# Attention on TensorE: all steady products in 64x32 tiles, scores and PV on opposite diagonals

## The chip, the cores and the metric

The kernel runs on one core of a Trainium2 chip. The metric is device time in microseconds (us); three runs of the kernel before gave a median of 669.69 us (669.62 to 669.82). One more execution was recorded by the hardware profiler, and all lines of a profile below come from such recorded executions. Engines are named as in the profile: PE is TensorE (PEld its weight loads), ACT is ScalarE, DVE is VectorE, POOL is GpSimd, SP is SyncE.

## The reference

```python
x  = A_x                                   # 1 x 2048 x 512, bf16
xn = layernorm(x)
q  = (xn @ wq) as 32 heads of 16;  k = xn @ wk;  v = xn @ wv     # one k and v for all heads
p  = softmax(q k^T * 16**-0.5);  s = concat_heads(p v) @ wo
g  = silu(silu(xn @ w1) @ w2)              # w1: 512 x 1792, w2: 1792 x 512
out = x + s * g
```

Each of the 32 heads has 2048 x 2048 scores. Their exponentials are the bulk of the work of the other engines, and the products around them the bulk of TensorE's.

## The kernel before, in words

**Order of work.** The kernel carries a planner (class `Planner`). A Python loop at build time holds a clock per engine, a time for each instruction and a latency for each pair of engines, and places the next instruction of the engine whose clock is earliest. `pe_step`, `act_step` and `generic_step` choose what that is. What comes out is one fixed list of instructions per engine, with semaphore waits where a buffer or an operand comes from another engine. On the chip each engine takes its list in order; the constants at the top of the file (`NPA`, `PRESS`, `A_LOW`, `SEEDS` and so on) only shape the lists.

**Scores.** The queries stand in 4 chunks of 512 and the heads in octets of 8. A q product gives `qt_sb`, 128 rows by 512 queries: 8 heads of 16 rows. A group `g` is half an octet (4 heads), 32 groups in all. `kt_sb[:, 0]` holds K with 16 live rows in each stripe of 32, `kt_sb[:, 1]` the same moved down by 16, so that a stripe's product picks one of its two heads. A score unit is one head by 128 keys by 512 queries: one matmul of 32 rows by 128 columns into a PSUM bank of its own (`s_mm`, L866). Up to four of them, in four row tiles, make a round (`do_S`). There are 2048 units. Banks 0 to 6 serve scores and other products, bank 7 (`OB`) holds the sum of PV.

**Exponentials.** A unit goes to one of two engines. ScalarE reads up to three adjoining banks in one instruction and writes exp to `pa_sb` (L1717). Or VectorE writes an integer form of the power of two to `db_sb` (L1002), from which GpSimd (L1202, four units in one instruction) or now and then VectorE (L1196) makes three shifted copies in `ds_sb`; the four copies, against four differently weighted copies of V, average out the error. So a VectorE unit costs PV four entries and a ScalarE unit one.

**PV.** An entry is 128 keys of one head: 128 rows by 32 columns (16 of V, 16 of ones for the denominator). Four heads' entries in four column tiles make a round (`do_pv`, L1282), all into bank 7. When a group's entries are done, VectorE transposes the bank (L1338), takes reciprocals and multiplies (L1341, L1342) and, after two groups, transposes back to `on_sb` (L1349).

**Products.** q, h (w1), z (w2) and w (wo) are jobs (`product`, L511): rounds of four column tiles, 128 rows by 32 columns, into one bank. A few of a job's rounds may be cut into 32x128 pieces that fill the fourth tile of a score round (L618). `gated` gives SiLU by a tanh on ScalarE (L669) and one VectorE instruction (L671). `final` and `store` end a 128-row tile of the output. The prologue transposes the normalized x (L527), makes K (`mk_K`, L553, evacuated at L565 and L567) and V (`mk_V`, L583, L592).

**Changes of form.** The planner counts `SWITCH` = 105 ns wherever TensorE passes from one tile form to another (`pe_start`). A score round ("S", 32x128) and the rounds of PV and jobs ("C", 128x32) are two forms. The last six units of the kernel are done in halves of 256 queries (`begin_halves`, L1667), so that the final normalization can begin on the first half.

```python
return pe.matmul(bank(b), lhsT=kt_sb[32 * i:32 * i + 32, g % 2, kt * P:(kt + 1) * P],      # a score unit
                 rhs=qt_sb[32 * i:32 * i + 32, (g // 2) % NQR, :],
                 start=True, stop=True, tile_position=(32 * i, 0))
...
h = pe.matmul(bank(OB)[32 * i:32 * (i + 1), cols], lhsT=lhs, rhs=rhs, start=s0, stop=s1,   # a PV entry
              tile_position=(0, 32 * i), skip_group_check=True)
```

Of the kernel before, what the change touches and what calls it, by code (L numbers as in the profile page):

```python
# [15 lines left out]
P = 128  # L16
# [5 lines left out]
SEEDS, STRETCH, SPREAD = (4812, 312, 1660, 4615, 1697, 8414, 4190, 8770, 5102, 5729), 64, 0.3  # L22
PIECE_MIN = {"z": 4, "h": 9, "q": 9, "w": 9}
# [3 lines left out]

T_P, T_SH, T_TR, T_AF = 600.0, 600.0, 630.0, 64.3
T_P64, DV_MIN, T_LIB = 1035.0, 40, 300.0
NPIECE = 1  # L30
HOLD_PO, URG_SPLIT = 300.0, 0
# [5 lines left out]


# [4 lines left out]
PH = []  # L43
# [4 lines left out]
BLG = 0  # L48
NEAR, AHEAD = 18, 0.6
SWITCH, SKEW = 105.0, 10.0  # L50
INF = float("inf")
DVE_LIMIT = 4000.0
MARGIN, MARGIN_END = 16, 20
TWO_LIMIT = 1300.0
HOLD, Q_LEAD = 1000.0, 3.3

LOW_USE, HIGH_USE, USE_WIN = 0.55, 0.8, 3000.0
S_TOL = 30.0
CLOSING, URGENT = 3, 1.5
NPA, PRESS = 26, 16  # L60
PRESS_Z, PRESS_H = 20, 16
PA_HI, DS_HI = 30, -1
NDB, NDS = 5, 8
STOL4 = 0.0
START_Z, START_H = 4, 8
EVAC = ()
LATE, QUEUE = 0.0, 10
Q3, Q4, J3, J4, N3, N4, SOLO = 10, -1, 1, 2, 1, 2, 0
END_DV = 40
RH, EVR, SC_PRIO, MT_EARLY = 6, (0, 2), 0, 1  # L70
METER, RATE, R0 = (), 1.0, 1.0
WIDE, NMIN, EARLY = 3, 3, 300.0
ONE_LIMIT = 2500.0
A_LOW, JOB_SPARE = 1000.0, 0


class Op:
    __slots__ = ("eng", "emit", "deps", "ports", "idx", "inc", "val", "t0", "end", "vis", "dma", "know", "sem", "waits", "mode", "ring")


class Task:
# [11 lines left out]
    (PE, AC): 221.0, (PE, DV): 221.0, (PE, PE): 0.0,  # L93
# [7 lines left out]
class Planner:  # L101

    def __init__(self):
        self.clk = {e: 0.0 for e in ENGINES}
        self.order = {e: [] for e in ENGINES}
        self.lastw = {}
        self.readers = {}
        self.tasks = {e: [] for e in ENGINES}
        self.mode = None
        self.dma_t = self.acc_t = 0.0  # L110
        self.last2 = {DV: None, PO: None}
# [29 lines left out]
    def place(self, eng, dur, emit, reads, writes, dma=0, t0=None, ports=1, after=None):  # L141
# [30 lines left out]
        self.order[eng].append(op)  # L172
        for k in reads:
            self.readers.setdefault(k, []).append(op)
# [5 lines left out]
    def set_mode(self, mode):  # L180
        self.mode = self.order[PE][-1].mode = mode
# [114 lines left out]
def bass_recurrent_scan__grouped_kv_mqa__dense_activation_silu__prompt_kernel(  # L296
# [20 lines left out]
    NKT = S // P  # L317
    SLOTS = 4 * NKT
# [8 lines left out]
    with ExitStack() as es:  # L327
# [12 lines left out]
        kt_sb = sb("kt_sb", [P, 2, S], BF16)  # L340
        v_sb = sb("v_sb", [P, K + 1, NKT, 48], BF16)
# [10 lines left out]
        tmp_sb = sb("tmp_sb", [P, 8, D], BF16)  # L352
# [6 lines left out]
        if EVAC:  # L359
            hs_sb = sb("hs_sb", [P, 2, NQ], BF16)  # L360
# [8 lines left out]
        zer_sb = sb("zer_sb", [P, NQ], BF16)  # L369
# [17 lines left out]
        PH.clear()  # L387
# [27 lines left out]
        pl.add(Task(DV, 550.0, lambda v: v.memset(zer_sb[:], 0.0), (), ["zer"], 0))  # L415
        pl.add(Task(DV, 435.0, lambda v: v.memset(wke_sb[:], 0.0), (), ["wke"], 0))
# [15 lines left out]
        for j in range(K + 1):  # L432
            pl.add(Task(PO, 660.0, lambda g, j=j: g.memset(v_sb[:, j, :, :], 1.0 if j == 0 else SHIFT_W[j - 1]),
                        (), [("V", j, c) for c in range(NC)], 3))
        pl.add(Task(PO, 1800.0, lambda g: g.memset(kt_sb[0:DH, 1, :], 0.0), [("xn", 3)], [("kt1", c) for c in range(NC)], 3,
                    gate=lambda: all(xn_task[t].op is not None for t in range(4))))
        pl.add(Task(AC, 1500.0, lambda a: a.activation(scr_sb[:, 0:1], scr_sb[:, 1:2], ACT.Exp), ["scr"], ["scr2"], 0))
        wke4 = wke_sb[:].rearrange("p c (i e) -> p c i e", e=32)
        pl.add(Task(AC, 300.0, lambda a: a.activation(
            wke4[:, :, :, 0:DH], wk_sb[:, :, :].unsqueeze(2).to_broadcast([P, NDC, 4, DH]), ACT.Copy),  # L440
# [59 lines left out]
        def job(kind, arg, pace, rounds, consume, preds=(), bk=None, mode="C", gate=None):  # L500
            jb = Job()
            jb.kind, jb.arg, jb.pace, jb.rounds, jb.consume = kind, arg, pace, rounds, consume
            jb.preds, jb.bank, jb.fixed, jb.mode, jb.gate = preds, bk, bk is not None, mode, gate
            jb.due, jb.pos, jb.end, jb.got, jb.left, jb.piece, jb.prev = None, 0, len(rounds), set(), len(rounds), None, None
            jb.tasks = {}
            jobs.append(jb)
            return jb
# [38 lines left out]
        def mk_K(c, ka, kb, bk=None):  # L546
# [13 lines left out]
            def consume(jb, op):  # L560
                b = jb.bank
                dst = kt_sb[:, 0, ka * P:kb * P]
                keys = [("kt0", k) for k in range(ka, kb)]
                if c == 0:
                    t = Task(AC, T_AF + 0.8333 * n, lambda a: a.activation(dst, bank(b)[:, 0:n], ACT.Copy), [("ps", b)], keys, 0)  # L565
                else:
                    t = Task(DV, T_P, lambda v: v.tensor_copy(dst, bank(b)[:, 0:n]), [("ps", b)], keys, 0)  # L567
                for k in range(ka, kb):
                    evac_kt[k] = t
                return [t]  # L570
# [5 lines left out]
        def mk_V(c):  # L576
            def rnd(k):
                def mk(b):
                    def emit(pe):
                        h = None  # L580
                        for t in (2 * k, 2 * k + 1):
                            for dc in range(NDC):
                                h = pe.matmul(bank(b)[:, t * DH:(t + 1) * DH],  # L583
                                              lhsT=xnT_sb[:, dc, (4 * c + t) * P:(4 * c + t + 1) * P],
                                              rhs=wv_sb[:, dc, :], start=(dc == 0), stop=(dc == NDC - 1))
# [4 lines left out]
            def consume(jb, op):  # L590
                b = jb.bank
                t = Task(DV, 400.0, lambda v: v.tensor_tensor(  # L592
                    v_sb[:, :, 4 * c:4 * c + 4, DH:2 * DH],
                    bank(b)[:, 0:4 * DH].rearrange("p (t e) -> p t e", e=DH).unsqueeze(1).to_broadcast([P, K + 1, 4, DH]),
                    wj_sb[:, :].unsqueeze(2).unsqueeze(3).to_broadcast([P, K + 1, 4, DH]), ALU.mult),
                    [("ps", b)] + [("wj", j) for j in range(K + 1)], [("V", j, c) for j in range(K + 1)], 0,
                    on_place=None)
# [3 lines left out]
            job("V", c, 0.0, [(rnd(k), ["wv"] + xnT_keys(c), 520.0) for k in range(2)], consume,  # L601
                bk=OB if c == 0 else None, mode="F", gate=lambda: xnT_ready(c))
# [4 lines left out]
        def product(jb, lhs, rhs, needs):  # L607
            n = len(jb.rounds)

            def rnd(k):  # L610
                def mk(b):
                    last = jb.left == 1
                    return lambda pe: col4(pe, b, lambda j: lhs(k, slice(0, P), 32 * j, 32), rhs(k, slice(0, P)), k == 0, last)
                return mk

            def piece(k, i, last):
                rows, b = slice(32 * i, 32 * i + 32), jb.bank
                return (lambda pe: pe.matmul(bank(b), lhsT=lhs(k, rows, 0, P), rhs=rhs(k, rows), start=False, stop=last,  # L618
                                             tile_position=(32 * i, 0), skip_group_check=True), needs(k))
            jb.rounds = [(rnd(k), needs(k), MM) for k in range(n)]  # L620
            jb.piece = piece

        def mk_q(oi):
            c, o = divmod(oi, NOC)

            def consume(jb, op):
# [7 lines left out]
                     gate=lambda: xnT_ready(c) and (oi < NQR or left_oct[oi - NQR] == 0))  # L634
            product(jb, lambda k, rows, a, n: wq_sb[rows, k, P * o + a:P * o + a + n],
                    lambda k, rows: xnT_sb[rows, k, c * NQ:(c + 1) * NQ], lambda k: ["wq"] + xnT_keys(c))

        def mk_q0(ta, tb, bk):
            n = (tb - ta) * P

            def rnd(t, dc):
                def mk(b):
                    def emit(pe):
                        for j in range(4):
                            h = pe.matmul(bank(b)[32 * j:32 * (j + 1), (t - ta) * P:(t - ta + 1) * P],
                                          lhsT=wq_sb[:, dc, 32 * j:32 * (j + 1)], rhs=xnT_sb[:, dc, t * P:(t + 1) * P],
# [15 lines left out]
        def gated(b, k, scale, dst, key, kind):  # L662
            src, held = bank(b), ("ps", b)
            t0 = None
            if kind in EVAC:
                src, held = hs_sb[:, k, :], ("hs", k)
                t0 = Task(DV, T_P, lambda v: v.tensor_copy(hs_sb[:, k, :], bank(b)), [("ps", b)], [held], 0,
                          [hs_last.get(k)])
            t1 = Task(AC, 490.0, lambda a: a.activation(t_sb[:, k, :], src, ACT.Tanh, scale=scale),  # L669
                      [held], [("t", k)], 0, [t0])  # L670
            t2 = Task(DV, T_P, lambda v: v.scalar_tensor_tensor(  # L671
                out=dst, in0=t_sb[:, k, :], scalar=1.0, in1=src, op0=ALU.add, op1=ALU.mult),
                [held, ("t", k)], [key], 0 if t0 is None else 1, [t1], ports=1 if t0 is None else 2)
            t2.first = [t1, t2] if t0 is None else [t0]
            if t0 is not None:
                hs_last[k] = t2
                pl.add(t1)
                pl.add(t2)
            return t2

        hs_last = {}

        def mk_h(c, ft, pace):
            def consume(jb, op):
# [3 lines left out]
                u_task[c, ft] = gated(b, k, 0.5, u_sb[:, ft, :], ("u", ft), "h")  # L688
# [6 lines left out]
        def mk_z(tt, pace):  # L695
            c, r = divmod(tt, 4)

            def consume(jb, op):
# [3 lines left out]
                tmp_task[tt] = gated(b, k, 0.25, tmp_sb[:, tt % 8, :], ("tmp", tt % 8), "z")  # L702
# [4 lines left out]
                and (tt < 8 or tt - 8 in fin_task and fin_task[tt - 8].op is not None))  # L707
# [1112 lines left out]
```

## Time and profile before

| | |
|---|---|
| median of 3 runs | 669.69 us (669.62 to 669.82) |
| span of the profiled execution | 667.9 us |
| granted TensorE clock, mean | 1.00 of full speed |
| DMA | 12.86 MB in all, mean 19 GB/s |

The span runs from the first to the last instruction. "Busy" is the time that at least one row of the engine covers; rows of one engine can overlap, since the next instruction starts before the last has left the pipeline, so a busy share says less than the distance from start to start. A group's row reads: line, engine, operation, out<-in, shape, count | busy us, mean ns of one | idle us before them, and what ended most of it. A matmul row lasts some 380 ns although the next round can start sooner.

The 40 slices show a start of some 15 us with GpSimd nearly idle, an even middle, and a short end:

```profile
DVE  8989999999899999989999899999999999998995
ACT  6999999999999999999999999999999999999997
POOL 3059889999898889998989888999899989897972
```

### The profile page before, as it was taken

How to read it: one execution, taken by the hardware profiler on the slowest of the kernel's cores; microseconds unless marked ns; L12 is line 12 of the kernel's file. 1: busy time of each engine (PE TensorE's matmuls, PEld its weight loads, DVE VectorE, ACT ScalarE, POOL GpSimd, SP SyncE). 2: the span in 40 equal slices, each digit the busy share in tenths (PEclk: the TensorE clock that was granted, in tenths of full speed). 3: DMA queues.
4: the chain of work that ended last, by engine and by line, in shares of the span. 5: the costliest groups of instructions: out<-in, count | busy, mean ns of one | idle time of the engine just before them, and what ended most of it. 6: DMA issues, size and time to landing. Idle time of an engine off the chain costs nothing.

```text
span 667.9 us, 21230 instructions
## 1 busy us (share of the span) xinstructions
PE 657.8 (98%) x8972; PEld 190.3 (28%) x8973; DVE 613.6 (92%) x1093; ACT 652.8 (98%) x767; POOL 561.9 (84%) x560
## 2 busy tenths in 40 slices
PE   8999999999999999999999999999999999999997
PEld 4322222222222222222222222222222322222222
DVE  8989999999899999989999899999999999998995
ACT  6999999999999999999999999999999999999997
POOL 3059889999898889998989888999899989897972
PEclk9999999999999999999999999999999999999999
DMA  9500000000000000000000010000000000000000
GB/s 302 164 9 2 3 1 2 2 3 2 1 2 18 19 18 18 1 2 2 2 2 2 18 32 18 2 2 2 2 2 2 2 18 18 17 18 2 2 2 33
DMA packets 11501, 12.86 MB, mean 19 GB/s; under 512 B 1808, under 2 KB 10768, under 8 KB 11408
## 3 DMA queue, kind: packets, MB, share of 16 engines
q1 hardware_dynamic: 10928, 10.78, 5.0%
q8 instruction: 72, 1.18, 0.7%
q0 software_dynamic: 192, 0.46, 0.2%
q10 hardware_dynamic: 288, 0.26, 0.1%
q14 instruction: 21, 0.17, 0.1%
HBM read 8.95 MB, written 2.10 MB: 17 GB/s over the span
## 4 chain that ended last, share of the span: by engine, by line
PE 88%; ACT 6%; DVE 4%; issue 1%; DMA 0%; ACTq 0%; DVEq 0%
PE ps L1282 38%; PE ps L866 29%; PE ps L511 20%; ACT pa_sb L1717 6%; DVE db_sb L1002 1%; DVE stats_sb L458 1%; ACT t_sb L669 1%; DMA ds_sb<-in_A_x_dram 0%; DVE fin_sb L719 0%; PE ps L527 0%; DVE xnT_sb L538 0%; DVE xn_sb L487 0%; DVE ob_sb L731 0%; DVE mv_sb L462 0%; DVE on_sb L1316 0%
## 5 line engine op out<-in xcount | busy, mean ns | idle before, releaser
L1717 ACT ACTIVATE pa_sb<-ps 128x1024 bf16<-128x1024 f32 (+2 forms) x670 | 617.0, 1027 | 4.8 <-PE ps L866 3.5
L1202 POOL INT64_ADD ds_sb<-db_sb x544 | 554.0, 1040 | 64.2 <-DVE otr_sb L1342 31.7
L1002 DVE TENSOR_SCALAR db_sb<-ps 128x512 uint16<-128x512 f32 x736 | 475.4, 683 | 40.0 <-PE ps L866 28.6
L1282 PE MATMUL ps<-ds_sb,v_sb 128*32 128x512 bf16 x2208 | 268.7, 383 | 0.0
L866 PE MATMUL ps<-qt_sb,kt_sb 32*128 32x512 bf16 x2048 | 251.2, 384 | 3.9 <-ACT pa_sb L1717 0.9
L1282 PE MATMUL ps<-pa_sb,v_sb 128*32 128x512 bf16 x1316 | 240.9, 382 | 0.0
L1282 PE MATMUL ps<-db_sb,v_sb 128*32 128x512 bf16 x736 | 169.3, 383 | 0.0
L866 PEld LDWEIGHTS ps<-qt_sb,kt_sb 32*128 32x128 bf16 x2048 | 62.8, 91 | 276.7 <-ACT pa_sb L1717 151.2
L1282 PEld LDWEIGHTS ps<-ds_sb,v_sb 128*32 128x32 bf16 x2208 | 65.6, 95 | 62.3 <-issue 44.6
L511 PE MATMUL ps<-xnT_sb,w_sb 128*32 128x512 bf16 x896 | 71.7, 383 | 0.0
L1282 PEld LDWEIGHTS ps<-pa_sb,v_sb 128*32 128x32 bf16 x1316 | 58.8, 95 | 37.9 <-issue 24.7
L511 PE MATMUL ps<-w_sb,u_sb 128*32 128x512 bf16 x820 | 64.1, 383 | 0.0
L1282 PEld LDWEIGHTS ps<-db_sb,v_sb 128*32 128x32 bf16 x736 | 42.2, 95 | 20.2 <-issue 14.7
L669 ACT ACTIVATE t_sb<-ps 128x512 bf16<-128x512 f32 x72 | 44.9, 623 | 0.0
L671 DVE SCALAR_TENSOR_TENSOR u_sb<-t_sb,ps 128x512 bf16<-128x512 bf16 x56 | 38.2, 683 | 1.0
L618 PE MATMUL ps<-w_sb,u_sb 32*128 32x512 bf16 x76 | 29.2, 384 | 0.0
L511 PEld LDWEIGHTS ps<-xnT_sb,w_sb 128*32 128x32 bf16 x896 | 17.1, 94 | 26.1 <-issue 21.1
L1359 POOL DMA_DIRECT2D kt_sb<-kt_sb x4 | 2.3, 566 | 23.9 <-DVE var_sb L481 8.1
L1338 DVE STREAM_TRANSPOSE f_sb<-ps 128x512 f32<-128x512 f32 x31 | 21.9, 706 | 0.0
L511 PEld LDWEIGHTS ps<-w_sb,u_sb 128*32 128x32 bf16 x820 | 15.2, 95 | 22.5 <-issue 19.3
L511 PE MATMUL ps<-wo_sb,on_sb 128*32 128x512 bf16 x256 | 18.9, 383 | 0.0
L511 PE MATMUL ps<-xnT_sb,wq_sb 128*32 128x512 bf16 x240 | 18.7, 384 | 0.1
(74 smaller groups left out, 180.8 us busy)
## 6 DMA issues: line engine op xcount, KB each, us to landing
w_sb<-in_B_w_dram SPq DMA_DIRECT2D x2, 1792.0 KB, 13.4
xr_sb<-in_A_x_dram SPq DMA_DIRECT2D x16, 128.0 KB, 2.6
out_dram<-ob_sb SPq DMA_DIRECT2D x16, 128.0 KB, 1.7
ds_sb<-in_A_x_dram SPq DMA_DIRECT2D x3, 512.0 KB, 6.6
wq_sb<-in_A_wq_dram SPq DMA_DIRECT2D x1, 512.0 KB, 4.9
wo_sb<-in_A_wo_dram SPq DMA_DIRECT2D x1, 512.0 KB, 16.2
kt_sb<-kt_sb POOLq DMA_DIRECT2D x4, 112.0 KB, 3.7
ds_sb<-in_A_x_dram ACTq DMA_DIRECT2D x2, 128.0 KB, 2.9
```

The lines of the kernel that those rows point to most:

```text
L458: ts_ = pl.add(Task(DV, 593.0, lambda v, t=t: v.bn_stats(stats_sb[:, t, :], x_tile(t)), [xkey(t)], [("st", t)], 1 + j, gate=(lambda j=j: S ...
L511: last = h.matmul(bank(b)[32 * j:32 * (j + 1), 0:n], lhsT=lhs(j), rhs=rhs, start=start, stop=stop, tile_position=(0, 32 * j), skip_group_c ...
L618: return (lambda pe: pe.matmul(bank(b), lhsT=lhs(k, rows, 0, P), rhs=rhs(k, rows), start=False, stop=last, tile_position=(32 * i, 0), skip ...
L669: t1 = Task(AC, 490.0, lambda a: a.activation(t_sb[:, k, :], src, ACT.Tanh, scale=scale), [held], [("t", k)], 0, [t0])
L671: t2 = Task(DV, T_P, lambda v: v.scalar_tensor_tensor(out=dst, in0=t_sb[:, k, :], scalar=1.0, in1=src, op0=ALU.add, op1=ALU.mult), [held, ...
L866: return pe.matmul(bank(b), lhsT=kt_sb[32 * i:32 * i + 32, g % 2, kt * P:(kt + 1) * P], rhs=qt_sb[32 * i:32 * i + 32, (g // 2) % NQR, :], ...
L1002: bt.P[i] = pl.add(Task(DV, T_P, lambda v: v.tensor_scalar(db_sb[:, bt.b, i * NQ:(i + 1) * NQ], bank(b), 128.0 * LOG2E, 128.0 * (SHIFT_BET ...
L1202: whole["po"].append(pl.add(Task(PO, T_P64, lambda g, cols=cols: g.int64_add(ds_sb[:, s, cols].bitcast(U64), db_sb[:, bt.b, cols].bitcast( ...
L1282: h = pe.matmul(bank(OB)[32 * i:32 * (i + 1), cols], lhsT=lhs, rhs=rhs, start=s0, stop=s1, tile_position=(0, 32 * i), skip_group_check=True)
L1338: t1 = pl.add(Task(DV, T_TR, lambda v: v.transpose(f_sb[:, k, :], bank(OB)), [("ps", OB)], [("F", k)], 1, [norm.get(("m", g - 2))]))
L1359: kt1[c] = pl.add(Task(PO, T_SWDGE, lambda e: e.dma_start(kt_sb[DH:P, 1, cols], kt_sb[0:P - DH, 0, cols]), [("kt0", k) for k in range(4 * ...
L1717: op = pl.place(AC, 0.8333 * NQ * n + T_AF, lambda a: a.activation(pa_sb[:, s * NQ:(s + n) * NQ].rearrange("p (b n) -> p b n", n=NQ), ps3[ ...
```

## The change

All steady products take tiles of 64 rows by 32 columns, eight of which fill the array: row halves at 0 and 64, columns at 0, 32, 64 and 96. The eight are used as two "lanes" of four. Lane 0 is tiles (0,0), (0,32), (64,64), (64,96); lane 1 is (64,0), (64,32), (0,64), (0,96). A step on a lane is four matmuls, a half round.

- A score unit is now two heads by 64 keys by 512 queries and takes lane 1 once: K is masked to one of the four heads in 64 rows (`part_sb`), and `kt_sb` holds two masked forms of each of its two versions. The wq columns are turned by 64 so that the output partitions match PV's rows.
- A PV entry is 64 keys of two heads, two matmuls of 64x32; two entries make a half round on lane 0.
- A product step is a half round on either lane. Both lanes add into the same bank, so a job does all its halves on one lane and then, after a wait of TensorE on itself (`SWAP` = 260 ns in the planner), those on the other.
- `tensor` replaces `set_mode` and `pe_start`: two clocks, one per lane, and starts that never go back. `pe_step` offers each free lane its work in turn: lane 1 first a score unit, lane 0 first PV or a job's half.
- ScalarE's exp takes one or two banks (`WIDE` = 2), and `choose_a` picks which free banks the next one or two score units go to.
- The pieces of 32x128, the filler matmuls and the halves at the end go. K's first chunk is evacuated by eight masked copies on ScalarE, each later chunk by two on VectorE; one DMA to the second version of K goes, and the other three carry twice as much. V is made in 64x64 tiles, twice over.
- `NPA` (exp buffers) goes from 26 to 21, the `tmp_sb` buffers from 8 to 4, `SEEDS` from ten values to none; most of the planner's other constants are replaced.

The core of the diff:

```diff
+    def tensor(self, mode, lane, dur, emit, reads, writes, t, after=None):
+        both = mode != "U"
+        free = max(self.lane) if both else self.lane[lane]
+        if self.mode not in (None, mode):
+            free = max(self.lane) + SWITCH
...
+        op = self.place(PE, dur, emit, reads, writes, t0=max(t, free, last.t0 if last else 0.0), after=after)
...
-        kt_sb = sb("kt_sb", [P, 2, S], BF16)
-        v_sb = sb("v_sb", [P, K + 1, NKT, 48], BF16)
+        kt_sb = sb("kt_sb", [P, 2, 2, S], BF16)
+        v_sb = sb("v_sb", [P, K + 1, NKB, 2 * DH], BF16)
...
+                for e in range(2 if c == 0 else 1):
+                    for a in range(2):
+                        dst = kt_sb[:, e, a, ka * P:kb * P]
...
+                            t = Task(AC, T_AF + 93.0 + 0.8333 * n, lambda g, dst=dst, e=e, a=a: g.activation(
+                                dst, bank(b)[:, 0:n], ACT.Copy, scale=part_sb[:, e, a:a + 1]), held, keys, 0, out[-1:] or parts)
...
-                        for t in (2 * k, 2 * k + 1):
+                        for t in range(4 * k, 4 * k + 4):
+                            kb = 8 * c + t
                             for dc in range(NDC):
+                                for r in (0, 64):
+                                    h = pe.matmul(bank(b)[r:r + 64, t * DH:(t + 1) * DH],
+                                                  lhsT=xnT_sb[:, dc, kb * 64:(kb + 1) * 64], rhs=wv_sb[:, dc, :],
...
+            def half(k, l):
...
+                    for j in range(4):
+                        r0 = 64 * (j // 2 ^ l)
+                        rows = slice(r0, r0 + 64)
+                        h = pe.matmul(bank(b)[32 * j:32 * (j + 1), :], lhsT=lhs(k, rows, 32 * j, 32), rhs=rhs(k, rows),
+                                      start=first, stop=last, tile_position=(r0, 32 * j), skip_group_check=True)
...
+        def s_half(b, g, i, kb):
+            def emit(pe):
+                for j in range(4):
+                    r0, k0 = 64 * (j // 2 ^ 1), 64 * kb + 32 * (j % 2)
+                    h = pe.matmul(bank(b)[32 * j:32 * j + 32, :], lhsT=kt_sb[r0:r0 + 64, g % 2, i, k0:k0 + 32],
+                                  rhs=qt_sb[r0:r0 + 64, g // 2 % NQR, :], start=True, stop=True, tile_position=(r0, 32 * j),
+                                  skip_group_check=True)
...
             def emit(pe):
+                for l in range(2):
+                    for (i, lhs, rhs, s0, s1) in mm:
+                        rows, q = slice(64 * l, 64 * l + 64), 64 * l + 32 * i
+                        h = pe.matmul(bank(OB)[q:q + 32, :], lhsT=lhs[rows], rhs=rhs[rows], start=s0, stop=s1,
+                                      tile_position=(64 * l, q), skip_group_check=True)
...
+        def do_half(l, t, jb):
+            k = jb.place[l]
+            op = pl.tensor("U", l, MM, jb.half(k, l), jb.needs(k), [("ps", jb.bank)], t, after=jb.prev if jb.lane == 1 - l else None)
...
-NPA, PRESS = 26, 16
...
-WIDE, NMIN, EARLY = 3, 3, 300.0
+NPA, NDB, NDS, NTM = 21, 5, 8, 4
...
+WIDE, PAIR_WAIT, GRP_WAIT = 2, 51.21, 116.171
```

## The prediction

> **What bounds the kernel now.** I read the page's busy table first, then the groups of instructions with the shapes kept apart, then the waits, then some microseconds of the timeline in the steady part, and last the starts of single instructions in the trace. The profiled execution spans 667.9 us; the median of the runs shown is 669.69, so 1.8 us lie around the span, and I add them at the end.
>
> ```profile
> PE 657.8 (98%) x8972; PEld 190.3 (28%) x8973; DVE 613.6 (92%) x1093; ACT 652.8 (98%) x767; POOL 561.9 (84%) x560
> ```
>
> Two engines show 98%. Neither figure says how much is work, since rows of one engine overlap. So I look at single forms and at starts.
>
> ```profile
> L1717 ACT ACTIVATE pa_sb<-ps 128x1024 bf16<-128x1024 f32 x622 | 588.5, 1048 | 4.1 <-PE ps L866 2.9
> L1002 DVE TENSOR_SCALAR db_sb<-ps 128x512 uint16<-128x512 f32 x736 | 475.4, 683 | 40.0 <-PE ps L866 28.6 <-PE ps L618 5.4 <-PE ps L1282 0.8
> ...
> L1717 ACT ACTIVATE pa_sb<-ps 128x512 bf16<-128x512 f32 x40 | 22.8, 623 | 0.7 <-PE ps L866 0.6
> ```
>
> A row lasts 1048 ns for two score banks and 623 for one. Start to start in the trace, a pair takes 905 ns (shortest 904, median 905, mean 932), a single 478, a triple 1331, a tanh (L669) 478: 427 ns per bank and 51 per instruction. So ScalarE's work from its first exp (start 11.37) to the end of its last (659.85) is 622 x 0.905 + 40 x 0.478 + 8 x 1.331 + 72 x 0.478 + 2.0 (the halves of L1667) = 629.1 us, in a window of 648.5: it **waits 19.4 us** in all, most of it inside rows, where the idle column doesn't show it.
>
> ```profile
> 301.83 0.10 PEld L866 LDWEIGHTS ps<-qt_sb,kt_sb 32*128 32x128 bf16 x3 [0.42 <-ACT pa_sb L1717]
> 301.84 0.39 PE L866 MATMUL ps<-qt_sb,kt_sb 32*128 32x512 bf16 x3
> 302.01 0.68 DVE L628 TENSOR_SCALAR qt_sb<-ps 128x512 bf16<-128x512 f32 x1
> 302.15 0.10 PEld L1282 LDWEIGHTS ps<-ds_sb,v_sb 128*32 128x32 bf16 x4 [0.23 <-issue]
> 302.16 0.40 PE L1282 MATMUL ps<-ds_sb,v_sb 128*32 128x512 bf16 x4
> 302.17 0.10 PEld L1282 LDWEIGHTS ps<-pa_sb,v_sb 128*32 128x32 bf16 x2
> 302.18 0.10 PEld L1282 LDWEIGHTS ps<-ds_sb,v_sb 128*32 128x32 bf16 x2
> 302.38 0.38 PE L1282 MATMUL ps<-pa_sb,v_sb 128*32 128x512 bf16 x2
> ```
>
> Two PV rounds start 0.22 us apart, but a score round and the PV round after it 0.32: a change of tile form costs about 0.106 us beyond the 0.216 of a round. Counted from 30 to 650 us, the starts of rounds are 952 times 0.222 apart within a form, 619 times 0.322 after a score round and 618 times 0.332 before one: 617 of 620 us. **TensorE is the bound**: rounds, and 1237 changes of form (131 us). Only some 12 us are waits (6 ns on each of the first kind, 10 on each of the last). Of the 641 score rounds 440 hold only 3 of 4 tiles.
>
> **The change on TensorE.** Counts of the changed program are read from the instructions it issues.
> - Form changes in the steady part go: 641 x 2 x 0.106 = -136 us.
> - A score unit takes four of eight tiles for one pass: 2048 half rounds, worth 1024 rounds against 641: 383 x 0.216 = +83 us.
> - PV (2150 half rounds on one diagonal) and the products (556 on each) come to 1631 rounds, against 1644 in the four-column form: nothing.
> - The diagonals aren't evenly fed. Matmuls start in program order, and 494 times two half rounds in a row are of one diagonal; laid out in order, 5310 half rounds need 2870 slots and not 2655: 215 x 0.216 = +46 us.
> - V takes 256 load-and-matmul pairs and not 64: at 0.034 each (L583, eight in 0.27) +6.5 us at most, about a quarter of it before the first exp.
>
> Sum: -1 us. I take the slot at the 0.2157 of the four-column rounds. No row shows the 64x32 form. From below: no mixed form can stream 512 columns faster than both forms shown, so there is no gain. From above: the 0.226 that a first follower takes after a form change, +10 ns on 2870 slots, 29 us; far above, half rounds that exclude each other, 5310 x 0.216 = 1147 us. I choose 0.2157, since both forms shown keep it with four streams, one with four streams per row and one with four outputs per column, and the new form needs four and two. Issue covers it: 64 pairs of L645 start 13.4 ns apart on average, and eight per slot need 107 of 216 ns.
>
> [...] The rows at 302.17 and 302.18 load for all 128 rows while the round of 302.16 runs, and the next round starts after 0.22, so the sum goes by the rows.
>
> **ScalarE.** The count of banks for exp hardly moves (1312 to 1300; VectorE takes 748 units and not 736), but pairs become rarer: 392 pairs and 516 singles, 908 instructions for 676. Work: 392 x 0.905 + 516 x 0.478 + 72 x 0.478 = **635.8 us, +6.7**.
>
> Start: eight masked copies of K in place of two (L565). With a pointer operand L451 lasts 722 against L446's 629, so +93: 4 x 0.252 and 4 x 0.465 us, all ahead of the first exp. From the first copy's 9.40: 1.0, then q 0.5, then 1.9, to 12.8; TensorE meanwhile does the first V (64 pairs, 1.7 to 2.2 us) before its first scores. First exp **13.1 for 11.4, +1.7**. Bounds: 0, if the 32 units that the first K chunk then gives (16 before) refund it from the early waits, and 2.5 with V at 0.034.
>
> End: the last six units are no longer done in halves; both half transposes (0.45 us, L1306) stand after the last PV, with reciprocals and products between. Slot end to end of span was 8.0 us; +0.9 makes 8.9.
>
> **ScalarE's waits** decide. I cut both programs, at ScalarE's order, into stretches, summed for each ScalarE's work and TensorE's slots up to the matmuls it needs, and added up where TensorE's sum is the larger. With 65 stretches (10 us each) the old program gives 19.9, against 19.4 measured, so this length stands for the buffering that seven banks give; the new gives 16.9. With 32: 11.7 and 7.1; with 16: 8.0 and 4.7. Scaled to the measured 19.4 that is 16.5 or 11.8; I take **15**, with 4.7 as the low end.
>
> 1649 of 2048 score half rounds wait at their head for a bank (855 on ScalarE, 794 on VectorE). Behind each stands, in order, the PV half of the other diagonal. It was so before, for nearly every score round:
>
> ```profile
> PEld ps L866 <- ACT pa_sb L1717: 151.2, 355, 0.7
> PEld ps L866 <- DVE db_sb L1002: 106.6, 240, 0.7
> PEld ps L1282 <- issue: 84.0, 371, 0.2
> ```
>
> 98 more waits are new, TensorE on itself, where a product changes its diagonal; other halves are written between, so nothing, or 98 x 0.38 (one matmul row) = 37 us without that cover.
>
> **Costed at nothing.** VectorE gets 12 units, 3 more K copies, a longer V copy and 4 fewer shifts: +8 us on 581 us (start to start), hidden by its own slack. POOL: 557 shifts for 544 at 1.015 us: 565 in the 616 us from its first (39.0) to its last, still 50 free. Both lose that cover only if the span fell below about 620. Fewer exp buffers (21 for 26) and tmp buffers (4 for 8) only bind if PV lags. The 84 filler matmuls go; the granted clock is 1.00 all through and TensorE has no long gap, so no gain, no loss.
>
> **Sum:** 13.1 + 635.8 + 15 + 8.9 = 672.8 us span, and 1.8 around it: **674.6 us**, 0.7% slower. The 136 us are spent again on half-filled score passes and idle slots; what is late next is ScalarE, with more instructions than before.
>
> **Rivals.**
> - *Two diagonals smooth the feed* (faster): a score half round no longer needs three free banks at once and never waits for a form change, so exps hardly wait. Price: waits of 4.7 and not 15, 664.3 us. It decides once ScalarE waits under 9 us, 10 ns per exp. For it: longer stretches balance better than before. Against it: 516 singles look like banks coming one at a time.
> - *The slot is not 0.2157* (slower): +10 ns makes TensorE's order 633 (619 slots, 14 of T, K, V) + 29 = 662 us, 26 over ScalarE's work: 13.1 + 662 + 4.7 + 8.9 + 1.8 = 690.5. For it: the new waits break the stream often, and a first follower takes 0.226. Against it: 952 rounds average 0.222, waits included.
> - *It doesn't do what it says*: the diagonals exclude each other, 1147 us of slots, about 1170. Against it: three or four tiles of each old form run beside each other.
>
> **Chances.** Forecast 0.52, smooth feed 0.28, dearer slot 0.17, excluded diagonals 0.03. A measurement of this kernel can tell some 0.2% from no change, 668.4 to 671.0. The forecast's waits of 9 to 24 us put 0.12 within that bound. Faster 0.27, same 0.13, slower 0.60. Range 663 (waits 4.7, the start refunded) to 692 (the dearer slot, with a little more wait); likeliest case alone 669 to 683.
>
> **What would show it.** Score and PV half rounds alternating at about 0.108 us with no 0.32 steps; if starts of one diagonal are 0.226 or more apart, the slot was wrong. First exp near 13.1. ScalarE start to start 478 and 905. The difference between its window and 635.8 is the wait: under 9 and I am wrong on the sign. If TensorE's row falls well below 95%, its slots weren't the rival of ScalarE that I take them for.

## The result, and the profile after

The changed kernel takes 680.63 us (median of 4 runs, 680.34 to 682.02) against 669.66 for the kernel before: ratio 1.0167, 95% interval 1.0153 to 1.0181. It is slower by 11.0 us, where the prediction had 4.9. The profiled execution spans 680.2 us and took 682.02, the slowest of the four; the other three span 678.4 to 678.9.

The busy row of the page, then the two forms of exp from the groups with the shapes kept apart (busy us, mean ns of one | idle us before them):

```profile
PE 670.4 (99%) x21773; PEld 353.9 (52%) x21774; DVE 624.3 (92%) x1116; ACT 661.1 (97%) x1005; POOL 576.1 (85%) x572
```

```profile
L1504 ACT ACTIVATE pa_sb<-ps 128x1024 bf16<-128x1024 f32 x392 | 403.0, 1097 | 0.5 <-PE ps L1187 0.4
L1504 ACT ACTIVATE pa_sb<-ps 128x512 bf16<-128x512 f32 x516 | 298.4, 686 | 4.0 <-PE ps L870 3.9
```

TensorE's share went up, not down. The exp rows have grown from 1048 and 623 ns although their columns haven't, and this turns out to be the key to the case. Now a microsecond of the steady part, TensorE only (start, duration, line, count):

```profile
300.77 0.39 PE L870 MATMUL ps<-qt_sb,kt_sb 64*32 64x512 bf16 x4
300.85 0.39 PE L1187 MATMUL ps<-ds_sb,v_sb 64*32 64x512 bf16 x4
300.98 0.39 PE L870 MATMUL ps<-qt_sb,kt_sb 64*32 64x512 bf16 x4
301.07 0.39 PE L1187 MATMUL ps<-ds_sb,v_sb 64*32 64x512 bf16 x4
301.20 0.39 PE L870 MATMUL ps<-qt_sb,kt_sb 64*32 64x512 bf16 x4
```

Score (L870) and PV (L1187) half rounds alternate; on one diagonal they start 0.21 to 0.22 us apart, without the steps of 0.32. From 60 to 655 us the median from start to start of one tile is 216 ns on both diagonals, as forecast.

The first exp of the kernel before and of the changed kernel:

```profile
11.37 5.48 ACT L1717 ACTIVATE pa_sb<-ps 128x1536 bf16<-128x1536 f32 x4
...
16.59 0.61 ACT L1504 ACTIVATE pa_sb<-ps 128x512 bf16<-128x512 f32 x1
```

Where the 12.3 us between the two profiled spans lie, in us. "Work" prices an instruction of ScalarE from row end to row end (0.490 us for one bank, 0.917 for two; the run row_ends below shows why), and "waits" is how much later than that the ends came:

| | before | after |
|---|---|---|
| first exp starts at | 11.4 | 16.6 |
| ScalarE's work from there to the last exp | 637.6 | 647.1 |
| its waits (after 60 us alone) | 11.0 (9.4) | 7.0 (2.0) |
| end of the last exp to end of the span | 7.8 | 9.4 |
| span | 667.9 | 680.2 |

So the change did smooth the feed of ScalarE: after 60 us it waits 2 us in all. But there were only 11 us of waits to win, and 232 more exps, a later start and a longer tail cost 16.3. These are parts of a sum, read from two profiles; the runs below ask what a part is worth when it alone is taken away, and that is mostly less.

### The profile page after: what moved, and what is told of

Same layout as the page of the kernel before. It is cut to its first block, busy times and chain, and to the rows that moved or that the text cites. A ratio compares the mean times of both kernels' runs of the same rounds, so it can differ in the third digit from the quotient of the medians.

```text
span 680.2 us, 46507 instructions
## 1 busy us (share of the span) xinstructions
PE 670.4 (99%) x21773; PEld 353.9 (52%) x21774; DVE 624.3 (92%) x1116; ACT 661.1 (97%) x1005; POOL 576.1 (85%) x572
## 4 chain that ended last, share of the span: by engine, by line
PE 95%; DVE 4%; issue 0%; ACT 0%; ACTq 0%
PE ps L870 43%; PE ps L1187 29%; PE ps L640 20%; DVE db_sb L946 1%; PE ps L541 1%; DVE stats_sb L473 1%; PE ps L525 0%; PE ps L567 0%; DVE part_sb L445 0%; DVE kt_sb L586 0%; PE ps L605 0%; ACT kt_sb L583 0%; PE ps L670 0%; DVE fin_sb L730 0%; ACTq L329 0%
## 5 line engine op out<-in xcount | busy, mean ns | idle before, releaser
L1504 ACT ACTIVATE pa_sb<-ps 128x1024 bf16<-128x1024 f32 (+1 forms) x908 | 628.4, 863 | 4.5 <-PE ps L870 3.9
L870 PE MATMUL ps<-qt_sb,kt_sb 64*32 64x512 bf16 x8192 | 551.0, 379 | 1.2 <-issue 0.5
L1187 PE MATMUL ps<-ds_sb,v_sb 64*32 64x512 bf16 x4488 | 385.2, 377 | 0.0
L1187 PE MATMUL ps<-pa_sb,v_sb 64*32 64x512 bf16 x2600 | 308.6, 378 | 0.0
L870 PEld LDWEIGHTS ps<-qt_sb,kt_sb 64*32 64x32 bf16 x8192 | 181.2, 90 | 207.7 <-ACT pa_sb L1504 100.0
L1187 PE MATMUL ps<-db_sb,v_sb 64*32 64x512 bf16 x1496 | 165.4, 377 | 0.1
L1187 PEld LDWEIGHTS ps<-ds_sb,v_sb 64*32 64x32 bf16 x4488 | 142.2, 91 | 21.0 <-issue 1.3
L640 PE MATMUL ps<-xnT_sb,w_sb 64*32 64x512 bf16 x1792 | 134.4, 378 | 0.0
L640 PE MATMUL ps<-w_sb,u_sb 64*32 64x512 bf16 x1792 | 125.0, 377 | 0.0
L1187 PEld LDWEIGHTS ps<-pa_sb,v_sb 64*32 64x32 bf16 x2600 | 91.8, 91 | 19.0 <-ACT pa_sb L1504 5.6
L1187 PEld LDWEIGHTS ps<-db_sb,v_sb 64*32 64x32 bf16 x1496 | 49.1, 91 | 9.9 <-DVE f_sb L1204 3.0
L640 PEld LDWEIGHTS ps<-w_sb,u_sb 64*32 64x32 bf16 x1792 | 43.1, 92 | 17.4 <-DVE db_sb L946 1.0
```

Source lines behind the costliest of these rows:

```text
L640: h = pe.matmul(bank(b)[32 * j:32 * (j + 1), :], lhsT=lhs(k, rows, 32 * j, 32), rhs=rhs(k, rows), start=first, stop=last, tile_position=(r ...
L870: h = pe.matmul(bank(b)[32 * j:32 * j + 32, :], lhsT=kt_sb[r0:r0 + 64, g % 2, i, k0:k0 + 32], rhs=qt_sb[r0:r0 + 64, g // 2 % NQR, :], star ...
L1187: h = pe.matmul(bank(OB)[q:q + 32, :], lhsT=lhs[rows], rhs=rhs[rows], start=s0, stop=s1, tile_position=(64 * l, q), skip_group_check=True)
L1504: op = pl.place(AC, 0.8333 * NQ * n + T_AF, lambda a: a.activation(pa_sb[:, s * NQ:(s + n) * NQ].rearrange("p (b n) -> p b n", n=NQ), ps3[ ...
```

## The experiments

Comparisons are with the changed kernel's 680.63 us (or 681.42 when it ran again, see after_again) or the 669.7 of the kernel before.

**row_ends: what does an exp cost?** ScalarE alone, `SINGLES, PAIRS = 64, 32`, nothing between the exps.

> A kernel that leaves out the whole computation and writes zeros: 64 exps of one bank and then 32 of two, start after start on ScalarE, with no wait between them and the other engines idle. In runs of 10 and 6, rows started 0.477 and 0.904 us apart but ended 0.490 and 0.917 apart. Theory (the ends are the pace; starts only run ahead of them, and not without limit): the 64 last 0.59 + 63 x 0.490 = 31.5 us from the first start to the last end, and start to start grows to 0.490 once the rows have grown long enough; the 32 pairs end 0.917 apart, 29.3 us in all. Rival (the forecast's price, 0.478 and 0.905 from start to start): 0.59 + 63 x 0.478 = 30.7 us and 28.9 us, rows that stop growing near 700 ns and ends that close up to 0.478.

The two groups in the timeline (start, time from the first start to the last end):

```profile
13.79 31.46 ACT L119 ACTIVATE pa_sb<-ps 128x512 bf16<-128x512 f32 x64 [0.48 <-PE ps L100]
44.37 30.22 ACT L121 ACTIVATE pa_sb<-ps 128x1024 bf16<-128x1024 f32 x32
```

The pairs start at 44.37, that is 30.58 us or 64 x 0.478 after the first single. But the 64 singles are done only after 31.46 = 0.597 + 63 x 0.490. Both numbers stand in the same two lines: **starts run 12.5 ns per instruction ahead of the ends**. Single rows grow from 591 ns at the second to 1366 at the 64th, the pairs from 1805 to 2192, with no limit in 96 instructions. The theory's price is right; its idea that the starts would soon be held back is wrong. An exp costs 427 ns per bank and 63 per instruction, not 51. So a long row here is a queue and not a slower exp: in the changed kernel the rows grew because ScalarE had nearly no pause to drain it, and its ends after 60 us lie only 2.0 us behind this price in all.

A row by itself is longer than that price: the second one's 591 ns less 427 leave 164, the distance from row end to row end leaves 63, and the sums here go by the 63.

**micro: do eight tiles at work lengthen an exp, and what held up part_sb?** First part: `v.tensor_scalar(o_sb[:, 0:2], in_sb[:], row_sb[:, 0:1], None, op0=ALU.mult)` and three others, each beside `g.memset(big_sb[:, k, :], 0.0)`, then alone. Second part: the six phases.

> A kernel that leaves out the whole computation and measures two things by themselves; its output is zeros. First part: beside a GpSimd memset of 128x2048 bf16 each, VectorE does an f32 128x2 tensor_scalar with a pointer operand, one with a constant, a tensor_tensor, and a bn_stats; then all four with GpSimd idle. Theory (GpSimd's memset held up the tensor_scalar of part_sb): the first lasts over 1 us, and 0.07 to 0.16 with GpSimd idle; bn_stats lasts 0.69 in both. Rival (the row_sb operand or its wait): under 0.2 us in both. Second part: ScalarE does 10 exps of one bank and 6 of two, start after start, in six phases: TensorE idle; four 128x32 column tiles; four 32x128 row tiles; one diagonal of 64x32 tiles; four 64x32 tiles in one half of the columns, two row halves; both diagonals. In the two kernels an exp's row lasted 623 and 1048 ns before, 686 and 1097 after, at the same distances from start to start (477 and 904). Theory A (eight tiles at work lengthen an exp's way to its end): rows near 623 and 1048 in the phases with four tiles, near 690 and 1100 with both diagonals. Theory B (two row halves that write the same PSUM partitions do it): the fifth phase is lengthened as well. Rival (the other engines do it): the same rows within 15 ns in all phases with TensorE at work. In each a slot takes 0.216 us from start to start; if both diagonals need more, the forecast's slot was too low.

```profile
1.81 1.65 DVE L55 TENSOR_SCALAR o_sb<-in_sb,row_sb 128x2 f32<-128x2 f32 x1 [0.32 <-POOL lit_sb L83]
3.65 1.73 DVE L56 TENSOR_SCALAR o_sb<-in_sb 128x2 f32<-128x2 f32 x1 [0.19 <-POOL lit_sb L83]
5.57 0.16 DVE L57 TENSOR_TENSOR o_sb<-in_sb 128x2 f32<-128x2 f32 x1 [0.19 <-POOL lit_sb L83]
7.35 0.69 DVE L58 BATCH_NORM_STATS2 st_sb<-r_sb 128x6 f32<-128x512 bf16 x1 [1.61 <-POOL lit_sb L83]
9.26 0.23 DVE L55 TENSOR_SCALAR o_sb<-in_sb,row_sb 128x2 f32<-128x2 f32 x1 [1.22 <-POOL lit_sb L86]
9.59 0.17 DVE L56 TENSOR_SCALAR o_sb<-in_sb 128x2 f32<-128x2 f32 x1
```

```profile
1.64 1.80 POOL L84 MEMSET big_sb<- 128x2048 bf16 x1
3.56 1.81 POOL L84 MEMSET big_sb<- 128x2048 bf16 x1
```

Beside GpSimd's memset a two-element tensor_scalar lasts to about the memset's end, with a pointer operand (1.81 + 1.65 = 3.46; 1.64 + 1.80 = 3.44) and without (3.65 + 1.73 = 5.38; 3.56 + 1.81 = 5.37); alone they take 0.23 and 0.17. The tensor_tensor and the bn_stats here take 0.16 and 0.69 beside a memset and alone. The theory holds. Why these two are not held up, the rows don't show.

Second part, the ten single exps with TensorE idle and with both diagonals at work:

```profile
13.98 5.00 ACT L119 ACTIVATE pa_sb<-ps 128x512 bf16<-128x512 f32 x10 [0.48 <-PE ps L100]
...
77.64 5.00 ACT L119 ACTIVATE pa_sb<-ps 128x512 bf16<-128x512 f32 x10 [2.05 <-PE ps L105]
```

The same 5.00 us, and the ten rows agree within 2 ns in all six phases. Theories A and B fall. The rival, the other engines, isn't tested, since VectorE and GpSimd were idle too; but ScalarE's rows grow here with all of them idle, so nothing from outside is needed. Both diagonals beside each other start four matmuls every 108.5 ns, a slot of 0.217: the dearer slot is out.

**products_short and tanh_one: which list sets the pace?** Same lists, less work on one engine.

```diff
+                        n = NQ if first else 64
-                        h = pe.matmul(bank(b)[32 * j:32 * (j + 1), :], lhsT=..., rhs=rhs(k, rows),
+                        h = pe.matmul(bank(b)[32 * j:32 * (j + 1), 0:n], lhsT=..., rhs=rhs(k, rows)[:, 0:n],
...
-            a.activation(t_sb[:, k, :], bank(b), ACT.Tanh, scale=scale)
+            a.activation(t_sb[:, k, 0:1], bank(b)[:, 0:1], ACT.Tanh, scale=scale)
```

> The changed kernel, all lists the same, but the q, h, z and w products stream only 64 of their 512 columns in every half round after a job's first; so most of these four products is left out. That takes 1013 of TensorE's 5310 half rounds down to a small part of their 0.216 us, some 90 us on each diagonal. Theory (since 60 us ScalarE's own instructions set the pace: measured from end to end, an exp of one bank takes 0.490 us and one of two 0.917, and its ends are later than that by 2.0 us in all after 60 us): nothing to gain from TensorE, 679 to 681.5 us. Rival (ScalarE waits for TensorE's slots, as the forecast's 15 us of waits had it): the waits go, 665 to 672 us.

680.43 us (679.13 to 681.57): some 90 us less on each diagonal bring 0.2 us, or 1.0 against 681.42, both within the scatter, so TensorE's slots alone don't set the pace. Yet the page's chain of waits says this, first of the changed kernel, then of products_short:

```profile
PE 95%; DVE 4%; issue 0%; ACT 0%; ACTq 0%
...
ACT 86%; PE 9%; DVE 4%; issue 1%; ACTq 0%
```

The two kernels take the same time, and the chain names another engine. In the changed kernel it follows overlapping 0.38-us rows back along TensorE without finding a gap; a share there isn't a bound.

> The changed kernel, all lists the same, but each of the 72 tanh on ScalarE does one column and not 512, so most of SiLU's tanh is left out: 72 x 0.426 = 31 us less work on ScalarE, spread over the kernel. Theory (ScalarE's instructions set the pace): the time falls by 8 to 31 us, 650 to 673 us; how far says how close the next engine stands behind. Rival (TensorE, VectorE or GpSimd set it): within 2 us of 680.6.

678.52 us (677.98 to 679.97): 2.1 less (2.9 against 681.42) for 31 us of work, far short of the theory's 8 and next to the rival's 2. By row ends ScalarE's waits rise from 7.0 to 34.4. So ScalarE's work isn't the only limit: something stands 2 to 3 us behind it. This kernel and the next two also clear `t_sb` at their start, one more GpSimd memset of 0.95 us; in the profiles of the next two the first exp then starts at 17.4 and 18.2, not at 16.6.

**both_short, three_short, replanned_short: what stands behind ScalarE?** both_short takes both edits above; three_short also cuts 54 of VectorE's SiLU products (`out=dst[:, 0:n]`, n = 1 after a buffer's first use). replanned_short is the kernel replanned, told of below, with the shorter products.

> The changed kernel, all lists the same, with both cuts at once: products of 64 columns after a job's first half round, and tanh of one column (most of these is left out). One cut alone gave 680.4 (TensorE, some 90 us less per diagonal) and 678.5 us (ScalarE, 31 us less). Theory (TensorE and ScalarE hold each other: a score half round waits for a bank from ScalarE, an exp for its scores, so only both together make room): 665 to 673 us. Rival (VectorE's list, or GpSimd's beside it, sets a pace within 2 us of ScalarE's): 676 to 679 us, as with the tanh alone.

674.43 us (673.60 to 675.33), between the two ranges and nearer the theory's. TensorE's cut, worth nothing alone, is worth 4.1 us once ScalarE is relieved. ScalarE still waits 30.0 us.

> The kernel "both_short" (products of 64 columns, tanh of one; 674.4 us, ScalarE's waits 30.0), and 54 of VectorE's 72 SiLU products on one column as well, some 28 us less work on VectorE; all lists the same, most of the products, the tanh and SiLU left out. Theory (VectorE's list is the third that holds the other two): 660 to 670 us. Rival (what is left is the wait from engine to engine, or GpSimd's list, and no engine's work): 673 to 675.5.

673.67 us (671.14 to 676.57): the rival, though the executions scatter more than the effect. No execution came to the theory's 670, so VectorE's list isn't the third limit. GpSimd's, the other half of the rival, was shortened in no run, so it stays possible. The waits of three_short (total us, times, longest) show what does remain on TensorE, score half rounds held at their head until a bank comes free:

```profile
PEld ps L878 <- ACT pa_sb L1512: 82.7, 294, 0.8
PEld ps L878 <- DVE db_sb L954: 51.7, 182, 0.8
```

> The kernel "replanned" (871 exps, ScalarE's work 641.9 us by row ends, its waits 13.2, 679.6 us), with the q, h, z and w products cut to 64 columns after a job's first half round (most of these products is left out), all lists as there. Theory (TensorE's list, with its waits in order, stands right behind ScalarE and takes up what ScalarE's shorter work gives): ScalarE's waits fall by 4 us or more and the time to 672 to 676. Rival (VectorE's or GpSimd's list takes it up): 678.5 to 680.5.

677.82 us (674.94 to 678.77), between the two; in the profiled execution, the fastest, ScalarE waits 7.6 us and not 13.2. TensorE's list takes up part of what ScalarE's shorter work offers in "replanned" (below); how much the scatter doesn't tell.

**parts_moved: what did the slow start cost?** The five instructions go behind the fourth bn_aggr, all other lists stay:

```diff
+        moved = [t.op for t in parts]
+        dv_list[:] = [op for op in dv_list if op not in moved]
+        k = dv_list.index(aggr[3].op) + 1
+        dv_list[k:k] = moved
```

> The changed kernel, but the five small instructions that build part_sb (L445 to L450) stand behind the fourth bn_aggr in VectorE's list, after GpSimd's memsets of v_sb; every other list is as it was. Theory (VectorE's first two of them were held up by GpSimd's memsets, 2.91 us for two, and the whole start with them): bn_stats begins near 3.4 us and not at 6.0, the first exp near 14.1 and not at 16.59 (2.9 less, 0.4 back for the five in their new place), and if the idle TensorE ahead of the first transposes was what halved its clock at 10.6 us, that half-clock stretch goes too and gives up to 1 us more: span 680.2 to 676.8 to 677.8. Rival (the start is slow because of what stands between the transposes and the first exp, and the waits after it take up what comes early): first exp earlier by under 1 us, or the span within 0.7 us of 680.2.

VectorE's start, first of the changed kernel, then of parts_moved:

```profile
2.74 2.91 DVE L445 TENSOR_SCALAR part_sb<-half_sb,row_sb 128x2 f32<-128x2 f32 x2
...
6.03 1.28 DVE L473 BATCH_NORM_STATS2 stats_sb<-ds_sb 128x6 f32<-128x512 bf16 x2
```

```profile
3.61 0.69 DVE L473 BATCH_NORM_STATS2 stats_sb<-ds_sb 128x6 f32<-128x512 bf16 x1 [0.87 <-DMA ds_sb<-in_A_x_dram]
...
6.13 0.20 DVE L445 TENSOR_SCALAR part_sb<-half_sb,row_sb 128x2 f32<-128x2 f32 x1
```

The stall is gone, the first exp starts at 14.32 and not 16.59, and the clock is full until the end. But the time is 680.44 us (679.92 to 681.14), 0.2 less than the changed kernel's first runs and 1.0 less than its later ones. Instruction by instruction, ScalarE's list is 3.1 us ahead at 60 us and 1.6 at 560, lost in some ten small steps. The theory was right on the start and wrong on its worth. Its span of 678.6 us meets neither range; both count from 680.2, the slowest execution of the changed kernel; against that kernel's other three (678.4 to 678.9) nothing is gained, as the rival had it.

**before_no_fillers: what did the fillers do?** The 84 fillers issue nothing (`op.emit = lambda pe: None`).

> The kernel before with its 84 filler matmuls left out, all lists otherwise the same (nothing of the result is left out). Theory (the fillers held TensorE's granted clock): the granted clock falls to 0.5 for at least one stretch of some 3.4 us between 10 and 50 us, and the time grows by 1 to 3 us, 670.7 to 672.7. Rival, which is the forecast (fillers cost and bring nothing): clock 1.00 throughout, 669.2 to 670.2.

670.35 us (669.71 to 671.27), ratio 1.0011 (1.0002 to 1.002). Busy time in stretches; PEclk is the third number from the end. First the kernel before, then without fillers, then the changed kernel:

```profile
10.00:15.00 5.00, 4.32 (x112) 2.40 (x100) 4.72 (x20) 4.82 (x6) 1.10 (x2) 1.00 1.05 396
15.00:20.00 5.00, 4.55 (x70) 2.15 (x67) 4.96 (x14) 4.22 (x5) 0.00 (x0) 1.00 1.09 367
```

```profile
10.00:15.00 5.00, 3.37 (x64) 1.39 (x52) 4.72 (x20) 4.86 (x6) 1.05 (x2) 0.90 1.05 396
15.00:20.00 5.00, 4.64 (x48) 2.34 (x46) 4.59 (x13) 3.61 (x5) 0.00 (x0) 0.76 1.08 365
```

```profile
10.00:15.00 5.00, 5.00 (x136) 4.05 (x138) 4.58 (x14) 3.27 (x9) 2.65 (x1) 0.66 1.04 398
...
25.00:30.00 5.00, 4.60 (x117) 2.82 (x113) 4.56 (x15) 3.73 (x7) 0.81 (x1) 0.76 0.17 49
```

Without fillers the clock halves once for 3.4 us (14.0 to 17.4) in the profile. Of the eleven executions the one with a mean clock of 1.00 took 669.71 us, as the kernel before does; eight with 0.996 or 0.997 took some 670.4 and the two with 0.995 some 671.3. The changed kernel's profile has it twice, at 10.5 and 27.6. The fillers do hold the clock (0.999 or 1.00 in all 21 executions with them), and a half-clock stretch costs 0.7 us here: the theory's mechanism, below its size.

**before_no_halves: the tail.** `RH` 6 to 0.

> The kernel before without the half-size exps at its end (the last six units are done whole), all lists the same up to there. From the last exp's slot end to the end of the span before took 8.0 us and the changed kernel 9.8. Theory (the lost halves are that difference): 9.6 to 10.0 us in place of 8.0, and 671.3 to 671.7 us in all. Rival (the forecast's +0.9): 8.9 us, 670.6. Second rival (the tail of the changed kernel is longer for another reason, its order of reciprocals and products): 8.0 to 8.3 us, within 0.4 us of 669.7.

670.38 us (670.33 to 671.21). From the end of the last exp to that of the span it takes 8.7 us, not 7.8: +0.95, the forecast's +0.9. The changed kernel's 9.4 holds 0.6 more that this doesn't explain.

**before_no_seeds: the order.** `SEEDS = ()` in the kernel before.

> The kernel before with SEEDS = () as in the changed kernel, one part of the change alone: the planner's thresholds aren't varied, and it lays out another order of the same instructions (673 exps and not 676). Theory (the order was one of many, and a good one): ScalarE's waits, 11.0 us by row ends in the kernel before, grow, and the time with them, 671 to 676 us. Rival (any order that the planner lays out does as well): 669 to 670.4.

673.96 us (673.72 to 674.10). The cost is right, the place isn't: ScalarE's waits are 11.5 us, as before, but the tail grows from 7.8 to 12.1, since this order leaves a z product for after the last exp. An order alone is worth 4 us, at its end.

**taf_back and replanned: a better order for the new form?**

```diff
-T_P, T_SH, T_TR, T_AF = 600.0, 600.0, 630.0, 52.0
+T_P, T_SH, T_TR, T_AF = 600.0, 600.0, 630.0, 64.3
```

> The changed kernel with one planner constant set back: T_AF 52 to 64.3, the price of an instruction of ScalarE beyond its columns. From row end to row end ScalarE takes 63 ns beyond its columns, from start to start 51. The order is laid out anew: 895 exps in place of 908, 401 pairs and 494 singles, ScalarE's work 645.1 us and not 647.1. Theory (the order was laid out for a ScalarE 12 us faster than it is, and a true price gives a better one): 1 to 3 us less than the changed kernel, 677.6 to 679.6. Rival (the share of work is as good with the wrong price): within 0.7 us of it, 680 to 681.3.

replanned has that, the parts held back behind the fourth bn_aggr, and other settings of the planner (its first four here):

```diff
+LEAD = 427.427
+FRAG = 2.064
+SLACK = 132.956
+A_HIGH = 4351.797
...
-                ["row"] + [("half", q, a) for q in range(4) for a in range(2)], [("part", e)], 0, [i2] + halfs)))
+                ["row"] + [("half", q, a) for q in range(4) for a in range(2)], [("part", e)], 0, [i2] + halfs,
+                gate=lambda: ("mv", 3) in pl.lastw)))
```

> The changed kernel's instructions in another order: T_AF 64.3, part_sb built behind the bn_aggr of tile 3, and nineteen thresholds of the planner chosen anew. 871 exps in place of 908 (421 pairs, 450 singles, 1292 units), ScalarE's work 641.9 us by row ends in place of 647.1. Theory (what the changed kernel lost is ScalarE's instruction count and its start): 5.2 us less work and a start 1 to 2 us earlier, 673.5 to 676 us; still above 669.7, since 641.9 is 4.3 more than the 637.6 of the kernel before, and start and tail are longer. Rival (the other lists hold ScalarE whatever its work, as the shortened tanh had it): 678 to 681 us.

taf_back 682.23 us (679.75 to 684.78), replanned 679.60 (678.26 to 681.87). replanned lies in its rival's range, the median of taf_back above both of its ranges. In the profiled executions ScalarE's work shrinks by 2.5 and 5.7 us, and its waits grow from 7.0 to 11.8 and 13.2: fewer exps alone don't pay. The clock goes with the time here, too. The two executions of taf_back at 1.00 took 679.8 us, the three at 0.995 to 0.997 took 682.2 to 684.8; those of replanned at 1.00 and 0.999 took 678.3 and 678.8, at 0.997 and 0.994 they took 680.4 and 681.9. No version here beats the kernel before.

**after_again: the spread.** The changed kernel once more, on another chip than parts_moved.

> The changed kernel itself once more, for its spread: four executions gave spans of 680.2, 678.4, 678.9 and 678.7 us, with mean clocks of 0.994 and 0.996 to 0.997; five of the kernel with part_sb built later 678.1 to 679.3. Theory (each half-clock stretch of 3.4 us early on costs some 0.7 us, as in the kernel before without fillers): 680.2 to 681 us in the median, and an execution with two stretches lies about 1 us above one with a single one. If the later part_sb gained more than 0.7 us, this median is above 681.

681.42 us (680.81 to 682.37), 0.8 above the first runs and above the theory's range. By the expectation's own test the later part_sb gained more than 0.7 us; but the two ran on different chips, and against the first runs it gained 0.2, so that isn't shown. These executions show a clock of 0.997 or 0.999 and scatter by 1.6 us without following it: what separates them is not settled.

## Why the prediction was wrong on the size

The direction was right, and the mechanism in the main: TensorE's form changes went, and ScalarE with more instructions is what runs without a pause (2.0 us of waits after 60 us). Not foreseen is that it isn't late alone, as tanh_one shows. Two terms of the sum were mis-sized, the start and the price of an instruction of ScalarE. As differences from the kernel before, in us, work and waits measured by row ends:

| | forecast | measured | missed |
|---|---|---|---|
| first exp | +1.7 | +5.2 | 3.5 |
| ScalarE's work | +6.7 | +9.5 | 2.8 |
| ScalarE's waits | -4.4 | -4.0 | 0.4 |
| tail | +0.9 | +1.6 | 0.7 |
| span | +4.9 | +12.3 | 7.4 |

The measured span is that of the slowest of four executions; in the medians 6.1 us were missed. Point by point:

- **TensorE: right.** No 0.32 steps, slots of 0.216, and its slots alone aren't the bound (products_short). The weight loads' rows last 90 to 92 ns on average, and the slot with them is 0.216. The rivals of a dearer slot and of diagonals that exclude each other are refuted. V's 64 pairs took 1.18 us, under the 1.7 to 2.2 allowed.
- **ScalarE's work: the step whose reading was wrong.** The prediction put it "427 ns per bank and 51 per instruction" and "635.8 us, +6.7". Read from start to start, that misses 12.5 ns per instruction (row_ends): the work is 647.1 us, 9.5 more than before, since 232 more exps at 63 ns cost 14.6 and 12 fewer banks give back 5.1. Of the 19.4 us of "waits" before, 8.4 were work; to these the prediction's stretches were scaled, and it gave the new kernel 15. By the same start-to-start measure the new kernel had 18.1 (a window of 653.9 less 635.8) and by row ends 7.0. That the change in waits came out near the forecast's is in part luck, then. Its first profile had the sign: rows of 1048 ns at starts 905 apart.
- **Smooth feed, the faster rival: half right.** Waits after 60 us fell from 9.4 to 2.0, as it said. It gave no gain, since the whole pool was 11.0 us and the extra instructions alone cost 9.5.
- **Start: the largest miss in the profile.** +1.7 forecast, +5.2 measured. The masked copies cost what was forecast (0.249 and 0.462 us from start to start, for 0.252 and 0.465). Missed were the 2.4 us by which the first transposes came later (9.95 for 7.58; 8.92 with part_sb moved), behind part_sb and GpSimd's memsets, and TensorE at half clock from 10.5 us on, for 3.4 us, with 2.0 us of idling ahead of the first transposes. Most of it isn't in the time, though: 2.3 us won back gave 0.2 to 1.0.
- **Fillers: wrong.** "No gain, no loss" is 0.7 us per half-clock stretch in the kernel before (before_no_fillers).
- **Tail:** the halves were priced right (+0.95 for +0.9); 0.6 more came on top.

So the terms say where the 12.3 us lie, and the price of an exp and the tail are shown by runs of their own; that ScalarE's extra instructions cause the loss is argued, not shown. No run adds exps to the kernel before, and taking work or a late start off the changed kernel gave back 2 to 3 us at most for a single engine. What stays open: which waits stand beside ScalarE, where less work of TensorE, ScalarE and VectorE together gave some 7 us and another order 1 to 2; what GpSimd's list and the fewer buffers (`NPA` 21 for 26, `tmp_sb` 4 for 8) have to do with it, which no run changes; and why the executions of the changed kernel scatter by 1 to 2 us and those of the kernel before mostly by 0.3. The clock goes with part of it in taf_back and replanned, and with none of it in after_again.

## What to carry to other kernels

Price an instruction of ScalarE from row end to row end in an unbroken run; here a row longer than the distance of its neighbours was a queue (up to 2192 ns at 905 apart in row_ends), and the "wait" that was computed from starts held work. Before a bound engine is relieved, work out how much the next one really waits: here that was the whole prize, 11 us, and any instruction added there comes off it. When several lists lie within a few us of each other, a cut on one engine shows little (here 0.2 and 2.1 us alone, 6.2 together); cut two at once before calling either of them the bound.

## What the hardware showed unexpectedly

- ScalarE's recorded starts ran ahead of its ends by 12.5 ns per instruction for 96 instructions on end, up to rows of 2192 ns for 905 ns of distance.
- A tensor_scalar on two elements lasted 1.65 us beside a GpSimd memset of 1.80, and 0.23 alone.
- TensorE's clock halved for 3.4 us without a long pause: ahead of 27.6 us its longest idle time in the 4.6 us before was 0.57; in parts_moved an idle time of 1.56 ahead of the first transposes left it full. What sets it off, these rows don't show.
